# A pooled attention and gated convolution kernel: prologue reordered, groups of one at first, keys in 128-row chunks, and DMA transposes in place of TensorE's from sequence 2 on

## The chip, the cores and the metric

One core of a Trainium2 chip runs the whole program. The metric is device microseconds of one execution, the median of several. A profiled execution of the same kernel gives the trace from which all rows below are taken. PE is TensorE, PEld its weight loads, DVE VectorE, ACT ScalarE, POOL GpSimd, SP SyncE.

## The reference

There are 8 sequences of 576 positions, 8 heads of 64. Keys and values are averaged over blocks of 8 positions, so that each head has 72 pooled keys. The attention output of all heads (512 columns) goes through a gated feed-forward part with a convolution over three neighbouring positions.

```python
k_p = k.reshape(B, H, Sp, 8, D).mean(axis=3)        # Sp = 72
v_p = v.reshape(B, H, Sp, 8, D).mean(axis=3)
scores = q @ k_p^T / sqrt(D);  attn = softmax(scores);  x = attn @ v_p   # heads side by side: 576 x 512
h = relu(x @ w_in)                                   # 576 x 1024
conv[s] = sum over k of conv_w[k] * h[s + k - 1]     # three taps, zero at both ends
out = (h * sigmoid(conv)) @ w_out                    # 576 x 512
```

## The kernel before

All products are in bf16 with float32 sums in PSUM. Sequences are handled in `groups`, `[[0], [1, 2], [3, 4], [5, 6], [7]]`. A load brings a sequence's q or k to 64 partitions (row p holds the nine positions 9p to 9p+8), so a pair fills 128 partitions. A group has 5 tiles of query rows if it is one sequence (four of 128 rows and one of 64) and 9 if it is a pair (the middle one has 64 rows of each).

Preparation of a group: `prep_k` (L153) multiplies the key rows by a 0/1 pooling matrix `pm` that GpSimd builds, 72 matmuls in two halves, and DVE casts the sums to `kT` (L163). `prep_q` (L196) turns the queries on TensorE in five pieces, copied by DVE to `qT` (L202, L206, L211). `prep_v` adds the eight rows of each value block in three DVE steps (L172, L176, L179) into `va`, with 72 pooled positions on partitions and a ninth-of-65 column that holds 8, which yields the row sums.

Attention of a tile is five steps, `STEPS`:

1. `att_scores`: four matmuls of two heads each into the PSUM tile `s_ps` (L234; the pool `s_psum` has one buffer), and the negated row maxima `negm` on DVE (L243).
2. `att_exp`: two matmuls of an identity add `negm` to the scores (L257), then ACT takes the exponential into `e_t` (L266).
3. `att_transpose`: TensorE turns `e_t` head by head, eight transposes into `e_ps` (L277), and DVE copies them to `eT_t` (L283).
4. `att_values`: eight matmuls, one for each head, into `o_ps` (L293), then DVE's reciprocal (L302) and product `x_t` (L304).
5. `att_out`: TensorE turns `x_t` in four blocks (`x_ps`, L319), ACT copies them into `xT_t` (L324), the layout that the feed-forward part reads.

Feed-forward of a sequence: for each of eight blocks `fb`, `ffn_in` (8 matmuls, `h_ps` L338, relu on ACT L345), `ffn_conv` (8 or 10 matmuls by diagonal weights `dw`, `c_ps` L392, tanh on ACT L401) and `ffn_gate` (DVE, L410 and L411). `ffn_out` takes a tile through eight matmuls of 512 columns (`o_out` L419), an ACT copy (L427) and two DMAs to `out` from the SP queue (L435).

The order on every engine is written out by hand. The prologue loads on the POOL queue (k and q of 0, v of 0, `w_in`, k and q and v of 1, k and q of 2, `w_out`, v of 2, then the next pair), prepares group 0, runs the five steps over its five tiles, prepares group 1 and both its values. After that a plan of `SLOTS = 24` slots for each sequence b mixes the feed-forward part of b with the attention of b + 1, the preparation of the group that begins at b + 2, and the `ffn_out` tiles of b - 1. `at(slot, order, f)` puts a step in a slot; each engine runs its instructions in that order. A tile's five steps stand two slots apart. The pools `big_psum` and `sm_psum` (two buffers each) hold `h_ps`, `c_ps`, `o_ps` and all the small ones.

Of the kernel before, what the change touches and what calls it, by code (L numbers as in the profile page):

```python
# [16 lines left out]
def kernel(  # L17
# [21 lines left out]
    P = 128  # L39
# [7 lines left out]
    SLOTS = 24  # L47

    groups = [[0], [1, 2], [3, 4], [5, 6], [7]]
# [5 lines left out]
    v_pool = ctx.enter_context(tc.tile_pool(name="vp", bufs=2))  # L55
    vt_pool = ctx.enter_context(tc.tile_pool(name="vt", bufs=1))
    qT_pool = ctx.enter_context(tc.tile_pool(name="qT", bufs=2))
    att_pool = ctx.enter_context(tc.tile_pool(name="att", bufs=3))
    xT_pool = ctx.enter_context(tc.tile_pool(name="xT", bufs=2))
# [10 lines left out]
    ident_f = const.tile([P, P], FP32, name="ident_f")  # L70
    pm = const.tile([P, C, 2, Sp], BF16, name="pm")
    w_in_sb = [const.tile([P, d_ff], BF16, name=f"w_in_sb{c}") for c in range(n_dmc)]
# [4 lines left out]
    va_ring = [const.tile([Sp, H, D + 1], BF16, name=f"va{i}") for i in range(4)]  # L77
    kT_ring = [const.tile([P, n_pairs, KW], BF16, name=f"kT{i}") for i in range(4)]

    q_t, k_t, v_t, va_t, qT_t, xT_t, gT_t, hT_t = {}, {}, {}, {}, {}, {}, {}, {}  # L80
# [20 lines left out]
    def load_v(b):  # L101
        v_t[b] = v_pool.tile([Sp, H, POOL * D], BF16, name="v_t")
        nc.gpsimd.dma_start(
            out=v_t[b], in_=v[b].rearrange("h (sp r) d -> sp h (r d)", r=POOL)
        )

    def load_group(g):
        for i in range(len(groups[g])):
            load_k(g, i)
            load_q(g, i)  # L110
            load_v(groups[g][i])


    def build_pool_matrix():
        nc.gpsimd.memset(pm, 1.0)
        for base, sign in ((0, 1), (POOL - 1, -1)):
            nc.gpsimd.affine_select(
                out=pm,
                in_=pm,
# [3 lines left out]
                pattern=[[sign, C], [-sign * C * TB, 2], [-sign * POOL, Sp]],  # L123
                channel_multiplier=sign * C,
            )

    def build_conv_weights():
        cps = sm_psum.tile([P, 3 * n_fb], FP32, name="cw_ps", tag="sm")
# [16 lines left out]
    def prep_k(g, half):  # L145
# [3 lines left out]
        for j in range(2):  # L149
            pr = 2 * half + j  # L150
            for c in range(C):
                for hh in range(2):
                    nc.tensor.matmul(  # L153
                        out=ps[hh * D:(hh + 1) * D, j, 0:n, :],
                        lhsT=k_t[g][0:rows, 2 * pr + hh, c * D:(c + 1) * D],
                        rhs=pm[0:rows, c, 0:n, :],
# [11 lines left out]
    def prep_v(b):  # L168
        vt = v_t[b]
        va = va_ring[b % 4]  # L170
        t1 = vt_pool.tile([Sp, H, 4 * D], BF16, name="vt1")
# [3 lines left out]
        t2 = vt_pool.tile([Sp, H, 2 * D], BF16, name="vt2")  # L175
        nc.vector.tensor_tensor(  # L176
            out=t2, in0=t1[:, :, 0:2 * D], in1=t1[:, :, 2 * D:4 * D], op=OP.add
        )
        nc.vector.tensor_tensor(  # L179
            out=va[:, :, 0:D], in0=t2[:, :, 0:D], in1=t2[:, :, D:2 * D], op=OP.add  # L180
        )
        va_t[b] = va

    def prep_q(g, pr):

# [297 lines left out]
    with tc.manual_schedule():  # L483
# [20 lines left out]
        for kT in kT_ring:  # L504
            nc.vector.memset(kT, 0.0)
# [55 lines left out]
```

## Time and profile before

| | |
|---|---|
| median of three runs | 321.84 us (321.68 to 322.76) |
| profiled execution | 324.01 us, span 322.2 us |
| PE busy | 276.5 us, 86% of the span, 3087 matmuls |
| PEld / DVE / ACT / POOL busy | 201.5 / 177.6 / 145.0 / 27.0 us |
| granted TensorE clock | 0.989 of full speed |
| moved by DMA | 26.17 MB, HBM read 32.52 MB |

Times are counted from the first instruction of the span. A busy time of PE counts each matmul with its pipeline, so what a group of matmuls really takes from PE is read from the start of one group to the start of the next. The idle time of an engine is put down to whatever ended it.

### The profile page before, as it was taken

The page shows a single profiled execution, that of the slowest core. Times are in us where ns is not written, and L with a number is a line of the kernel's source. Part 1 is how long each engine was busy: PE and PEld are TensorE (multiplying, and loading weights), DVE is VectorE, ACT ScalarE, POOL GpSimd, SP SyncE. Part 2 cuts the span into 40 slices and gives each one's busy share as a digit, 9 for nine tenths or more (in the row PEclk, how much of TensorE's full clock was granted, in tenths as well). Part 3 has the DMA queues.
Part 4 walks back from the last instruction along what each step waited for, and adds up shares of the span by engine and source line. Part 5 has one row for each costly group of instructions (what it writes and reads, how often), then busy time and mean ns, then how long its engine had stood idle before and what let it go on. Part 6 is the DMA issues. An engine that isn't in the chain of part 4 may idle for free.

```text
span 322.2 us, 7171 instructions
## 1 busy us (share of the span) xinstructions
PE 276.5 (86%) x3087; PEld 201.5 (63%) x3087; DVE 177.6 (55%) x402; ACT 145.0 (45%) x240; POOL 27.0 (8%) x42
## 2 busy tenths in 40 slices
PE   0528782998999999998999999999999999989994
PEld 0526572786667666776676666766676677656651
DVE  3846558486387745655687636643864466432210
ACT  0022300465644455655544365556454556546442
POOL 8732004100020100000000000000000000000000
PEclk9999998799999999999999999999999999999999
DMA  7899999993139693111161121111102111302335
GB/s 108 110 198 181 170 191 144 175 177 64 35 41 185 106 194 68 35 33 35 35 108 33 37 56 30 43 40 33 34 16 54 33 35 35 67 2 65 67 67 112
DMA packets 22195, 26.17 MB, mean 81 GB/s; under 512 B 3196, under 2 KB 17044, under 8 KB 22164
## 3 DMA queue, kind: packets, MB, share of 16 engines
q0 software_dynamic: 16368, 16.26, 37.1%
q1 hardware_dynamic: 5796, 9.45, 12.9%
q8 instruction: 24, 0.39, 0.5%
q14 instruction: 7, 0.06, 0.1%
HBM read 32.52 MB, written 9.44 MB: 130 GB/s over the span
## 4 chain that ended last, share of the span: by engine, by line
PE 67%; DMA 13%; ACT 9%; DVE 5%; POOL 3%; issue 2%; ACTq 0%; POOLq 0%
PE h_ps L338 18%; PE o_out L419 17%; PE c_ps L392 16%; DMA v_t<-in_v_dram 9%; PE e_ps L277 5%; ACT tg_t L401 4%; DMA w_in_sb<-in_moe_w_in_dram 4%; ACT hT_t L345 3%; PE s_ps L234 3%; PE q_ps L196 2%; PE s_ps L257 2%; PE k_ps L153 2%; DVE gT_t L411 2%; PE x_ps L319 2%; DVE tg_t L410 1%
## 5 line engine op out<-in xcount | busy, mean ns | idle before, releaser
L338 PE MATMUL h_ps<-xT_t,w_in_sb 128*128 128x288 bf16 x512 | 75.4, 288 | 4.8 <-ACT xT_t L324 3.6
L419 PE MATMUL o_out<-w_out_sb,gT_t 128*128 128x512 bf16 (+1 forms) x296 | 70.9, 380 | 0.6
L345 ACT ACTIVATE hT_t<-h_ps 128x576 bf16<-128x576 f32 x64 | 41.6, 650 | 55.2 <-PE h_ps L338 54.1
L392 PE MATMUL c_ps<-hT_t,dw 128*128 128x288 bf16 (+4 forms) x560 | 58.3, 249 | 6.8 <-ACT hT_t L345 4.3
L338 PEld LDWEIGHTS <-w_in_sb 128*128 128x128 bf16 x512 | 48.3, 98 | 20.3 <-issue 5.8
L392 PEld LDWEIGHTS <-dw 128*128 128x128 bf16 x560 | 44.7, 98 | 17.6 <-issue 6.6
L401 ACT ACTIVATE tg_t<-c_ps 128x576 bf16<-128x576 f32 x64 | 41.7, 651 | 28.2 <-PE c_ps L392 27.4
L419 PEld LDWEIGHTS <-gT_t 128*128 128x128 bf16 (+1 forms) x296 | 26.9, 98 | 31.3 <-DVE gT_t L411 4.5
L427 ACT COPY osb_t<-o_out 128x512 f32<-128x512 f32 (+1 forms) x37 | 21.6, 585 | 46.2 <-PE o_out L419 46.2
L243 DVE TENSOR_REDUCE negm<-s_ps 128x8 bf16<-128x576 f32 (+1 forms) x37 | 27.8, 752 | 24.7 <-PE s_ps L234 24.5
L410 DVE TENSOR_SCALAR tg_t<-tg_t 128x576 bf16<-128x576 bf16 x64 | 19.5, 304 | 39.5 <-ACT tg_t L401 39.3
L283 DVE COPY eT_t<-e_ps 72x1024 bf16<-72x1024 bf16 (+1 forms) x37 | 24.8, 671 | 29.5 <-PE e_ps L277 29.4
L266 ACT ACTIVATE e_t<-s_ps 128x576 bf16<-128x576 f32 (+1 forms) x37 | 24.0, 650 | 16.5 <-PE s_ps L257 16.4
L411 DVE TENSOR_TENSOR gT_t<-tg_t,hT_t 128x576 bf16<-128x576 bf16 x64 | 29.3, 458 | 2.2
L304 DVE TENSOR_TENSOR x_t<-o_ps,r_t 128x512 bf16<-128x512 f32 (+1 forms) x37 | 25.6, 691 | 1.3
L277 PE MATMUL e_ps<-ident,e_t 128*72 128x128 bf16 (+1 forms) x296 | 24.4, 230 | 1.4 <-ACT osb_t L427 1.3
L257 PE MATMUL s_ps<-negm,ident 128*128 128x288 bf16 (+1 forms) x74 | 16.7, 311 | 10.2 <-DVE negm L243 10.2
L324 ACT COPY xT_t<-x_ps 128x512 bf16<-128x512 bf16 (+1 forms) x37 | 21.2, 572 | 5.5 <-PE x_ps L319 5.5
L277 PEld LDWEIGHTS <-e_t 128*72 128x72 bf16 (+1 forms) x296 | 20.3, 122 | 2.8 <-issue 1.7
L234 PE MATMUL s_ps<-kT,qT_t 128*128 128x144 bf16 (+1 forms) x160 | 16.9, 241 | 3.6 <-ACT e_t L266 3.6
L302 DVE RECIPROCAL r_t<-o_ps 128x8 f32<-128x8 f32 (+1 forms) x37 | 7.6, 206 | 18.4 <-PE o_ps L293 17.9
L293 PE MATMUL o_ps<-va,eT_t 72*128 72x65 bf16 (+1 forms) x320 | 17.4, 201 | 0.1
(38 smaller groups left out, 189.7 us busy)
## 6 DMA issues: line engine op xcount, KB each, us to landing
out_dram<-osb_t SPq DMA_DIRECT2D x72, 128.0 KB, 2.4
v_t<-in_v_dram POOLq DMA_DIRECT2D x8, 576.0 KB, 9.8
k_t<-in_k_dram POOLq DMA_DIRECT2D x7, 576.0 KB, 15.7
q_t<-in_q_dram POOLq DMA_DIRECT2D x7, 576.0 KB, 18.5
w_in_sb<-in_moe_w_in_dram POOLq DMA_DIRECT2D x4, 256.0 KB, 11.5
w_out_sb<-in_moe_w_out_dram POOLq DMA_DIRECT2D x1, 1024.0 KB, 26.3
k_t<-in_k_dram POOLq DMA_DIRECT2D x2, 288.0 KB, 4.5
q_t<-in_q_dram POOLq DMA_DIRECT2D x2, 288.0 KB, 5.2
```

The lines of the kernel that those rows point to most:

```text
L234: nc.tensor.matmul(out=sp[lo:hi, pr // 2, (pr % 2) * KW:(pr % 2 + 1) * KW], lhsT=qT_t[g][:, pr, t * P + lo:t * P + hi], rhs=kT_ring[b % 4] ...
L243: nc.vector.tensor_reduce(out=negm[0:rows], in_=sp[0:rows, :, 0:2 * KW].rearrange("p a (h s) -> p a h s", s=Sp), axis=AX.X, op=OP.max, neg ...
L266: nc.scalar.activation(out=e[0:rows], in_=sp[0:rows, :, 0:2 * KW], func=ACT.Exp, scale=1.0 / (POOL * 8.0))
L277: nc.tensor.transpose(out=ps[:, h, 0:rows], in_=e[0:rows, h // 4, (h % 4) * Sp:(h % 4 + 1) * Sp], identity=ident[0:rows, 0:rows],)
L283: nc.vector.tensor_copy(out=eT[:, :, 0:rows], in_=ps[:, :, 0:rows])
L304: nc.vector.tensor_tensor(out=x[0:rows].rearrange("p (a h d) -> p a h d", a=2, d=D), in0=ov[:, :, :, 0:D], in1=r[0:rows].unsqueeze(3).to_b ...
L338: nc.tensor.matmul(out=hps[:, j, 0:SC], lhsT=w_in_sb[dc][:, fb * P:(fb + 1) * P], rhs=xT_t[g][:, dc, i * S + j * SC:i * S + (j + 1) * SC], ...
L345: nc.scalar.activation(out=hT_t[b][:, fb, :].rearrange("p (a s) -> p a s", a=2), in_=hps[:, :, 0:SC], func=ACT.Relu, scale=0.5,)
L392: nc.tensor.matmul(out=cps[:, j, lo - j * SC:hi - j * SC], lhsT=dw[:, kk, fb, :], rhs=hT[:, fb, src:src + hi - lo], start=(kk == 1), stop= ...
L401: nc.scalar.activation(out=tg.rearrange("p (a s) -> p a s", a=2), in_=cps[:, :, 0:SC], func=ACT.Tanh, scale=0.5)
L411: nc.vector.tensor_tensor(out=gT_t[g][:, fb, i * S:(i + 1) * S], in0=tg1, in1=hT_t[b][:, fb, :], op=OP.mult)
L419: nc.tensor.matmul(out=ops_[0:rows, :], lhsT=gT_t[g][:, fb, t * P:t * P + rows], rhs=w_out_sb[:, fb, :], start=(fb == 0), stop=(fb == n_fb ...
```

## The change

Groups are `[[0], [1], [2], [3], [4, 5], [6, 7]]`. The loads stand in another order on the POOL queue and are spread over the plan. The exponentials of a tile lie in one 640-column row (eight heads of 72 and 64 zero columns) and are turned in five chunks of 128 pooled keys; values lie likewise in five chunks of 128 rows, with three masked copies, so that a chunk's matmul writes all heads that it meets. From sequence 2 on (`E_DMA`, `X_DMA`) both turns are `dma_start_transpose` on the SP queue. The first sequence's scores use two PSUM tiles in turn. The matmuls of sequence 0's `ffn_in` go by halves of the sequence. The plan's slots are other ones.

```diff
+    NJ = 5
+    KP = NJ * P
+    E_DMA = 2
+    X_DMA = 2
-    groups = [[0], [1, 2], [3, 4], [5, 6], [7]]
+    groups = [[0], [1], [2], [3], [4, 5], [6, 7]]
...
-    va_ring = [const.tile([Sp, H, D + 1], BF16, name=f"va{i}") for i in range(4)]
+    v_ring = [const.tile([P, NJ, POOL * D], BF16, name=f"v{i}") for i in range(2)]
+    vm_ring = [const.tile([P, NJ, 3, D + 1], BF16, name=f"vm{i}") for i in range(4)]
+    e_ring = [const.tile([P, KP], BF16, name=f"e{i}") for i in range(4)]
     kT_ring = [const.tile([P, n_pairs, KW], BF16, name=f"kT{i}") for i in range(4)]
...
     def load_v(b):
-        v_t[b] = v_pool.tile([Sp, H, POOL * D], BF16, name="v_t")
+        rows = v[b].rearrange("h (sp r) d -> (h sp) (r d)", r=POOL)
+        vt = v_ring[b % 2]
         nc.gpsimd.dma_start(
-            out=v_t[b], in_=v[b].rearrange("h (sp r) d -> sp h (r d)", r=POOL)
-        )
-    def load_group(g):
-        for i in range(len(groups[g])):
-            load_k(g, i)
-            load_q(g, i)
-            load_v(groups[g][i])
-    def build_pool_matrix():
-        nc.gpsimd.memset(pm, 1.0)
+            out=vt[:, 0:4, :], in_=rows[0:4 * P].rearrange("(j p) x -> p j x", p=P)
+        )
+        nc.gpsimd.dma_start(out=vt[0:TB, 4, :], in_=rows[4 * P:])
...
+    def build_head_mask():
+        nc.gpsimd.memset(mask, 1.0)
+        for base, sign in ((Sp, 1), (-1, -1)):
+            nc.gpsimd.affine_select(
+                out=mask,
+                in_=mask,
+                compare_op=OP.is_ge,
+                fill=0.0,
+                base=base,
+                pattern=[[sign * (P - 2 * Sp), NJ], [-sign * Sp, 3]],
+                channel_multiplier=sign,
+            )
+        for vm in vm_ring:
+            nc.vector.tensor_scalar(
+                out=vm[:, :, :, D], in0=mask, scalar1=float(POOL), scalar2=None, op0=OP.mult
...
-        vt = v_t[b]
-        va = va_ring[b % 4]
-        t1 = vt_pool.tile([Sp, H, 4 * D], BF16, name="vt1")
+        vt = v_ring[b % 2]
...
+        t3 = vt_pool.tile([P, NJ, D], BF16, name="vt3")
         nc.vector.tensor_tensor(
-            out=va[:, :, 0:D], in0=t2[:, :, 0:D], in1=t2[:, :, D:2 * D], op=OP.add
-        )
-        va_t[b] = va
+            out=t3, in0=t2[:, :, 0:D], in1=t2[:, :, D:2 * D], op=OP.add
+        )
+        nc.vector.tensor_tensor(
+            out=vm_ring[b % 4][:, :, :, 0:D],
+            in0=t3.unsqueeze(2).to_broadcast([P, NJ, 3, D]),
+            in1=mask.unsqueeze(3).to_broadcast([P, NJ, 3, D]),
+            op=OP.mult,
...
+            copy = nc.scalar.copy if g == 0 and pr % 2 else nc.vector.tensor_copy
+            copy(out=qT[:, pr, 0:8 * TB].rearrange("p (c t) -> p c t", t=TB), in_=ps[:, :, 0:TB])
...
-        sp = s_psum.tile([P, 2, 512], FP32, name="s_ps")
+        if g == 0 and t % 2:
+            sp = big_psum.tile([P, 2, 512], FP32, name="s_ps", tag="big")
+        else:
+            sp = s_psum.tile([P, 2, 512], FP32, name="s_ps")
...
-        e = att_pool.tile([P, 2, 2 * KW], BF16, name="e_t")
+        e = e_ring[tile_no[g, t] % 4]
         nc.scalar.activation(
-            out=e[0:rows], in_=sp[0:rows, :, 0:2 * KW], func=ACT.Exp, scale=1.0 / (POOL * 8.0)
+            out=e[0:rows, 0:4 * KW].rearrange("p (a x) -> p a x", a=2),
+            in_=sp[0:rows, :, 0:2 * KW],
+            func=ACT.Exp,
+            scale=1.0 / (POOL * 8.0),
...
-        ps = sm_psum.tile([Sp, H, P], BF16, name="e_ps", tag="sm")
-        for h in range(H):
+        eT = eT_pool.tile([P, NJ, P], BF16, name="eT_t")
+        a["eT"] = eT
+        if groups[g][0] >= E_DMA:
+            nc.sync.dma_start_transpose(out=eT[:, :, 0:rows], in_=e[0:rows, :])
+            return
+        ps = sm_psum.tile([P, NJ, P], BF16, name="e_ps", tag="sm")
+        for j in range(NJ):
             nc.tensor.transpose(
-                out=ps[:, h, 0:rows],
-                in_=e[0:rows, h // 4, (h % 4) * Sp:(h % 4 + 1) * Sp],
+                out=ps[:, j, 0:rows],
+                in_=e[0:rows, j * P:(j + 1) * P],
                 identity=ident[0:rows, 0:rows],
             )
-        eT = att_pool.tile([Sp, H, P], BF16, name="eT_t")
-        nc.vector.tensor_copy(out=eT[:, :, 0:rows], in_=ps[:, :, 0:rows])
-        a["eT"] = eT
+        copy = nc.scalar.copy if g == 0 else nc.vector.tensor_copy
+        copy(out=eT[:, :, 0:rows], in_=ps[:, :, 0:rows])
...
-            for h in range(H):
+            for j, x0, x1, first in (
+                (0, 1, 3, True), (1, 0, 3, False), (2, 0, 1, False),
+                (2, 1, 3, True), (3, 0, 3, False), (4, 0, 1, False),
+            ):
+                h = 2 * j - 1 + x0
+                kk = P if j < 4 else TB
                 nc.tensor.matmul(
-                    out=o[lo:hi, h // 4, (h % 4) * (D + 1):(h % 4 + 1) * (D + 1)],
-                    lhsT=eT[:, h, lo:hi],
-                    rhs=va_t[b][:, h, :],
-                    start=True,
-                    stop=True,
+                    out=o[lo:hi, h // 4, (h % 4) * (D + 1):(h % 4 + x1 - x0) * (D + 1)],
+                    lhsT=eT[0:kk, j, lo:hi],
+                    rhs=vm_ring[b % 4][0:kk, j, x0:x1, :],
+                    start=first,
+                    stop=(j == 4 or (j == 2 and x0 == 0)),
+                    skip_group_check=True,
...
+        if groups[g][0] >= X_DMA:
+            nc.sync.dma_start_transpose(
+                out=xT_t[g][:, :, t * P:t * P + rows], in_=a["x"][0:rows, :]
+            )
+            return
...
+    def ffn_in_half(b, j, f2):
+        g, i = where[b]
+        if b not in hT_t:
+            hT_t[b] = hT_pool.tile([P, n_fb, S], BF16, name="hT_t")
+            gT_t[g] = gT_pool.tile([P, n_fb, 2 * S], BF16, name="gT_t")
+        hps = big_psum.tile([P, 2, 512], FP32, name="h_ps", tag="big")
+        for f in range(2):
+            fb = 2 * f2 + f
+            for dc in range(n_dmc):
+                nc.tensor.matmul(
+                    out=hps[:, f, 0:SC],
+                    lhsT=w_in_sb[dc][:, fb * P:(fb + 1) * P],
+                    rhs=xT_t[g][:, dc, j * SC:(j + 1) * SC],
+                    start=(dc == 0),
+                    stop=(dc == n_dmc - 1),
...
+        if b == 0:
+            for j in range(2):
+                for f2 in range(n_fb // 2):
+                    at(w + 4 * j + f2, 0, ffn_in_half, b, j, f2)
+            for r in range(n_fb):
+                at(w + 6 + 2 * r, 0, ffn_conv, b, r)
+                at(w + 7 + 2 * r, -1, ffn_gate, b, r)
...
+            e_dma, x_dma = groups[ng][0] >= E_DMA, groups[ng][0] >= X_DMA
+            first = 5 if b == 0 else 0
+            m4 = 6 if e_dma else 5
+            steps = (0, 2, 2 if e_dma else 3, m4, m4 if x_dma else m4 + 2)
+            gap = (22.9 - first - steps[4] - (3 if x_dma else 0)) / (len(ts) - 1)
             for n, t in enumerate(ts):
-                s = w + int(n * gap)
+                s = w + first + int(n * gap)
                 for m, f in enumerate(STEPS):
-                    at(s + 2 * m, 1 + (4 - m), f, ng, t)
-        lead = [g2 for g2 in range(1, len(groups)) if groups[g2][0] == b + 2]
-        for g2 in lead:
-            for half in range(2):
-                at(w + 8 + 2 * half, 7, prep_k, g2, half)
-            for n2 in range(n_pairs + 1):
-                at(w + 12 + 2 * n2, 7, prep_q, g2, n2)
-            for n2, b2 in enumerate(groups[g2]):
-                at(w + 7 + 8 * n2, 8, prep_v, b2)
-            if g2 + 1 < len(groups):
-                at(w + 23, 9, load_group, g2 + 1)
+                    at(s + steps[m], 1 + (4 - m) if not (m == 2 and e_dma or m == 4 and x_dma) else 6,
+                       f, ng, t)
+            if ni == 0:
+                for n2, b3 in enumerate(groups[ng]):
+                    at(w + (7 if b == 0 else 1 + 2 * n2), 8, prep_v, b3)
+        for g2 in range(1, len(groups)):
+            b2 = groups[g2][0]
+            if b2 == b + 2:
+                for half in range(2):
+                    at(w + 11 + 2 * half, 7, prep_k, g2, half)
+                for n2 in range(n_pairs + 1):
+                    at(w + 14 + 2 * n2, 7, prep_q, g2, n2)
+            if b2 == b + 3 and g2 > 2:
+                for n2, b3 in enumerate(groups[g2]):
+                    at(w + 6 + 8 * n2, 9, load_k, g2, n2)
+                    at(w + 9 + 8 * n2, 9, load_q, g2, n2)
+        if b >= 3 and i == 0:
+            for n2, b3 in enumerate(groups[g]):
+                at(w - 2 * SLOTS + 2 + 6 * n2, 9, load_v, b3)
...
     with tc.manual_schedule():
         load_k(0, 0, slice(0, 4))
         load_k(0, 0, slice(4, 8))
         load_q(0, 0, slice(0, 4))
         nc.sync.dma_start(out=cw_raw, in_=moe_conv_w.rearrange("k (fb p) -> (k fb) p", p=P))
+        load_q(0, 0, slice(4, 8))
         make_identity(nc, ident)
-        build_pool_matrix()
-        make_identity(nc, ident_f)
-        load_q(0, 0, slice(4, 8))
+        nc.vector.memset(warm, 0.0)
+        nc.scalar.activation(out=warm, in_=warm, func=ACT.Exp)
+        for v0 in v_ring:
+            nc.vector.memset(v0[TB:P, 4, :], 0.0)
+        build_pool_matrix(True)
         load_v(0)
         for c in range(n_dmc):
             nc.gpsimd.dma_start(out=w_in_sb[c], in_=moe_w_in[c * P:(c + 1) * P, :])
+        for kT in kT_ring:
+            nc.vector.memset(kT, 0.0)
+        build_conv_weights()
+        build_head_mask()
+        for e in e_ring:
+            nc.vector.memset(e[:, 4 * KW:], 0.0)
         load_k(1, 0)
         load_q(1, 0)
         load_v(1)
-        load_k(1, 1)
-        load_q(1, 1)
+        build_pool_matrix(False)
+        for half in range(2):
+            prep_k(0, half)
+        for pr in range(n_pairs + 1):
+            prep_q(0, pr)
+        load_k(2, 0)
+        load_q(2, 0)
         nc.gpsimd.dma_start(
             out=w_out_sb, in_=moe_w_out.rearrange("(fb p) d -> p fb d", p=P)
         )
-        for kT in kT_ring:
-            nc.vector.memset(kT, 0.0)
-        for va in va_ring:
-            nc.vector.memset(va, float(POOL))
-        build_conv_weights()
-        prep_k(0, 0)
-        prep_k(0, 1)
-        for pr in range(n_pairs + 1):
-            prep_q(0, pr)
-        prep_v(0)
         ts = tiles_of[0]
-        for s in range(len(ts) + 4 + len(ts)):
+        for s in range(len(ts) + 4):
             for m in reversed(range(5)):
-                n, odd = divmod(s - m, 1)
-                if 0 <= n < len(ts):
-                    STEPS[m](0, ts[n])
-        for half in range(2):
-            prep_k(1, half)
-        for pr in range(n_pairs + 1):
-            prep_q(1, pr)
-        prep_v(1)
+                if 0 <= s - m < len(ts):
+                    STEPS[m](0, ts[s - m])
+            if s == 1:
+                prep_v(0)
+            if s == 4:
+                for half in range(2):
+                    prep_k(1, half)
+            if s > 4:
+                prep_q(1, s - 5)
+        prep_q(1, n_pairs)
         load_v(2)
-        prep_v(2)
-        load_group(2)
         for key in sorted(plan):
```

## The prediction

> **What bounds the kernel now.** I read four views in this order: the span in forty slices, the chain that ended last, PE's order of time in a steady stretch, and PE's waits. The slices say that there are two stages.
>
> ```profile
> PE   0528782998999999998999999999999999989994
> PEclk9999998799999999999999999999999999999999
> ```
>
> One digit is 8.1 us. PE is full from slice 8 (about 57 us) to the last slice but one, and half idle before. The chain of the first 60 us says why the full stretch starts there:
>
> ```profile
> 23.70 29.82 DMA v_t<-in_v_dram
> ...
> 53.55 1.23 DVE vt L172
> ...
> 55.95 0.68 DVE negm L243
> ...
> 56.66 0.64 PE s_ps L257 x2
> 57.30 1.92 PE h_ps L338 x8
> ```
>
> The load of sequence 2's values lands at 53.5 us; `prep_v(2)` waits for it on DVE, and behind it in DVE's order stands the `negm` that the first interleaved tile needs. PE reached its feed-forward part at 49.43 us, did 1.3 us of it and stood. It resumes at 56.66, so the stage counts from 55.4. The eight matmuls of 57.30 take 1.92 us; the same group takes 0.99 later, since the granted clock is 0.50 from 54 to 60 us.
>
> In the steady stretch what a group takes from PE is the distance to the next start (start, duration, engine, line):
>
> ```profile
> 96.14 0.90 PE L392 MATMUL c_ps<-hT_t,dw 128*128 128x288 bf16 x8
> 96.88 0.42 PE L293 MATMUL o_ps<-va,eT_t 72*128 72x65 bf16 x8
> 97.23 1.32 PE L153 MATMUL k_ps<-pm,k_t 128*64 128x144 bf16 x36
> 98.48 0.42 PE L257 MATMUL s_ps<-negm,ident 128*128 128x288 bf16 x2
> 98.74 1.14 PE L338 MATMUL h_ps<-xT_t,w_in_sb 128*128 128x288 bf16 x8
> 99.72 0.39 PE L319 MATMUL x_ps<-ident,x_t 128*128 128x128 bf16 x4
> ...
> 101.36 0.62 PE L277 MATMUL e_ps<-ident,e_t 128*72 128x128 bf16 x8
> 101.81 1.89 PE L419 MATMUL o_out<-w_out_sb,gT_t 128*128 128x512 bf16 x8
> 103.53 0.41 PE L234 MATMUL s_ps<-kT,qT_t 128*128 128x144 bf16 x4
> ```
>
> So c 0.74, values 0.35, half a pair's keys 1.25, negm 0.26, h 0.98, x turn 0.23 to 0.31, e turn 0.45 to 0.53 (other places), out 1.73, scores 0.25 to 0.35. Groups follow each other without gaps: PE is the bound. What it waits for after the resumption is little, 12.6 us in all (waiter, releaser, us, times, longest):
>
> ```profile
> PE c_ps L392 <- ACT hT_t L345: 4.3, 11, 0.5
> PE h_ps L338 <- ACT xT_t L324: 3.6, 7, 0.6
> PE c_ps L392 <- DVE x_t L304: 2.2, 4, 0.5
> PE e_ps L277 <- ACT osb_t L427: 1.3, 3, 0.4
> ```
>
> **Prologue: 55.4 becomes 37.** The first scores come at 16.64 us. They follow the kT casts, which DVE does after 24 `dw` products. After the change DVE has some 2.7 us more of small fills ahead of the casts, but starts the products 3.5 us earlier, since the identity that they wait for no longer follows GpSimd's pooling matrix: I leave 16.64. Before, the first `negm` waits for `prep_v(0)` (and that for the values, landed 18.5) and ends at 21.57; now it precedes it and ends at 17.75. From 21.57 to the last xT copy's end, 41.40, five tiles take 19.8 us. In this stretch 3.6 us of PE waits for ACT's exponential to free the one score buffer go, as the tiles alternate between two; the table load of 1.3 us is done in advance; `prep_v(0)` now keeps back the first values (+1.8 of its 2.3 us). Sequence 1's keys and queries now stand between the tiles: 5.1 us of PE by the rows of sequence 0 (2.37 and 2.73), half of it in PE's idle time (PE is busy 13.9 of the 20 us from 20 to 40): +2.6. Sum 17.75 + 19.8 - 3.6 - 1.3 + 1.8 + 2.6 = 37.05. Below: rounds paced by ACT alone (0.65 + 0.65 + 0.58 a tile), nine of them from 16.64, 33.6. Above: no step shortened and all of the preparation exposed, 21.57 + 19.8 + 5.1 = 46.5. The pair's separate preparation, both `prep_v` and the wait for `v_t` leave the path. The transfers cover this: sequence 1's queries are the seventh of 590 KB-sized pieces in a queue that brought 4.0 MB by 28 us, before they are used. GpSimd's second pooling matrix (two of 1.41 us) now stands ahead of the loads of sequence 2; megabytes queued before it hide it, and without that cover it would cost 2.8 us of a landing that is not wanted until slot 11. Gain 18.4, and the stretch at half clock (0.38 + 0.93 + about 0.3 in its groups): 1.6.
>
> **PE work.** The turns of 28 tiles leave PE: 28 x (0.48 + 0.26) = 20.7 us (19.0 by the shortest distances, 28.6 by the full durations 0.62 and 0.40). Sequence 1's five tiles turn five chunks instead of eight: 5 x 3 x 0.057 = 0.9. Values: six matmuls of 780 columns for eight of 520; at 288 columns in 0.122 us that is 0.33 for 0.35, nothing. Against it: sequences 2 and 3 are prepared singly (3.1 each by sequence 7's: two halves of 0.7, four pieces of 0.37, one of 0.24), so preparations after the prologue are 2 x 3.1 + 2 x 5.0 for 5.0 + 5.0 + 3.1: +3.1. One tile more (38 for 37): 0.86 and an `ffn_out` of 1.73: +2.6. Net -15.9. DVE's 28 copies of 0.685 and ACT's 28 of 0.584 go too, at no gain of their own: neither is the bound (55% and 45%). `ffn_in` of sequence 0 by halves is the same 64 matmuls.
>
> **Waits.** Of the 12.6 us those tied to the removed turns go (3.6 + 2.2 + 1.3): -7.1. In their place comes the landing of a DMA transpose, which no row shows. Nearest is the same queue's `out` transfer, 128 KB against 164 KB (e) and 131 KB (x):
>
> ```profile
> DMA to landing us min/median/max: 2.2/2.4/9.6
> ```
>
> (us from issue to landing of the 72 `out` transfers.) I take 3.0, near the median, with one neighbour's issue (0.51) ahead of it; ends 2.2 and 9.6. On SP, queued behind each transpose's wait for ACT or DVE, are the `out` pairs and the next tile's transposes, 56 more issues beside 72. From the changed program's order, priced by the distances above, I sum the PE work between a tile's negm matmuls and its value matmuls: eight of the 28 tiles have 2.9 to 3.3 us, the others 4.0 to 7.7, mean 4.6. The chain there is exponential 0.65, ACT's queue and signals 0.35, landing 3.0: 4.0. It is short in the eight, by 6.7 us together. The turned x must be there for the next sequence's `ffn_in`: six such joints have 2.5 to 4.8 us of cover against 0.21 + 0.69 + 0.1 + 3.0 = 4.0; short by about 2.0. New waits 8.7.
>
> [...]
>
> Sum against the profiled execution: 322.2 - 18.4 - 1.6 - 15.9 - 7.1 + 8.7 = 287.9 us of span, 289.7 with the 1.8 around it. The profiled execution lies 2.2 above the median of the runs, so 287.5, say 288.
>
> **Rivals.** (1) The prologue is bound by arrival and chain, not by what I took off: PE's stage starts at 46.5, time 298. For it: the DMA engines are busy without a break from 8 to 72 us in the slices. Against: what is needed first is loaded first. (2) The transposes land in 4 us, as SP's queue holds them up: chain 5.0, shortfall 19.5 at the values and 5 at the joints for 8.7: 304. (3) Slower: the transposes are the bound. One mechanism: each landing beyond PE's cover stops PE in its order, tile by tile. At a landing of 4.6 us (chain 5.6) the shortfalls are 32 and 9 us, the gain of 34 is used up and the time is as before; at 6 us they are 69 and 17, and the time is 365. For it: the transposes share the queue with 72 transfers, one of which took 9.6. Against: the median of 2.4. That the turns do not leave PE is ruled out: of 37 groups of e turns the changed program has 10.
>
> **Chances.** Forecast as it stands (277 to 296) 0.62; rival 1 0.13; rival 2 0.13; slower 0.11; no change 0.01. Faster by over 0.3%, which is about what a measurement can tell here: 0.88. The range's low end takes a prologue of 34, the turns at their full durations and no e shortfall: 288 - 3 - 4 - 4 = 277. Its high end takes in rival 1 with some late transposes and half of rival 2: 306. Left out are slower and half of rival 2.
>
> **What would show it.** Right: PE full from slice 5; `v_t` gone from the chain; no L277 or L319 group after about 90 us; transposes landing in 2.4 to 3.5 us; PE's waits on them under 10 us. Wrong: value matmuls waiting for `eT_t` a microsecond or more in most tiles; SP's transposes taking over 2 us each to issue; a first `ffn_in` after 45 us.

## The result and the profile after

The changed kernel takes 332.89 us (median of 331.33 to 337.43), the kernel before 322.30 beside it: a ratio of 1.031, 95% interval 1.024 to 1.037. It is slower; 288 was predicted. The profiled execution took 331.33 us, span 329.5, granted clock 0.963 (0.989 before). An execution more than 1.5% above the fastest of its kernel counts as slow and is left out of the ratios, not of the medians.

The span in forty slices, 8.2 us each:

```profile
PE   1569968880999752999797998999788889999994
PEclk9999999996799995899979999999999999999999
```

PE is busy from slice 4 on, as predicted, but has holes in slices 10, 15 to 16 and 22, and a smaller one in 20. The clock is 0.50 from 76.4 to 86.6 us and from 124.2 to 134.4, in and behind the first two holes, and from 165.1 to 168.5, behind the one in slice 20. The chain that ended last (start, us, what) names the three large holes:

```profile
34.93 5.99 PE h_ps L414 x48
...
72.18 9.92 DMA eT_t<-e
...
117.81 11.56 DMA eT_t<-e
...
170.13 6.54 DMA eT_t<-e
```

The feed-forward part starts at 34.93 us, and `v_t` is gone from the chain. In its place stand e turns of 6.5 to 11.6 us where 3.0 was counted. PE's waits (waiter, releaser, us, times, longest) agree:

```profile
PE o_ps L339 <- DMA eT_t<-e: 24.9, 9, 9.6
PE o_out L495 <- DVE gT_t L487: 6.5, 3, 2.3
...
PE o_ps L339 <- DVE eT_t L325: 2.1, 1, 2.1
```

Before, all of PE's waits after the resumption were 12.6 us; here they are 40.0 from 35.5 us on. The landings of the e turns (26 of the 28 have one in the trace), min, median and max:

```profile
DMA to landing us min/median/max: 2.3/2.6/14.4
```

The median is what was predicted. The long ones stand together, and POOL's timeline shows beside what (the e turns on SP are issued at 72.18 and 74.0, and land after 9.9 and 10.8 us):

```profile
67.53 0.68 POOL L96 DMA_DIRECT2D q_t<-in_q_dram  x1 [10.70 <-PE q_ps L228]
68.19 0.68 POOL L105 DMA_DIRECT2D k_t<-in_k_dram  x1
...
70.38 0.77 POOL L113 DMA_DIRECT2D v<-in_v_dram  x1 [0.83 <-DVE vt L198]
```

The plan's slots don't spread the loads: POOL has nothing else to do and issues each as soon as its buffer is free, which is when the preparation of the group before ends. That is also when the next sequence's first tile is turned. Set beside the loads in flight, the 26 e turns fall into two kinds: 19 with no load in flight have a median of 2.6 us (one is over 4), and seven beside loads have 2.9 to 14.4, median 9.9.

The windows of 74, 76 and 84 us (stretch, length, busy us of PE, PEld, DVE, ACT, POOL, granted clock, DMA share, GB/s) show what follows:

```profile
74.00:76.00 2.00, 0.28 (x3) 0.00 (x0) 0.25 (x1) 0.65 (x1) 0.00 (x0) 1.00 1.15 223
76.00:78.00 2.00, 0.00 (x0) 0.00 (x0) 0.00 (x0) 0.00 (x0) 0.00 (x0) 0.60 1.18 225
...
84.00:86.00 2.00, 2.00 (x10) 1.14 (x9) 0.82 (x3) 0.65 (x1) 0.00 (x0) 0.50 0.37 77
```

From 76 to 78 us all four engines stand while the DMA engines move 225 GB/s (DMA share 1.18), and when PE resumes at 82.15 us it runs four microseconds at half clock, to 86.6.

The second and third of the waits above come from VectorE's order. In the trace of after, around the end of sequence 1's stage:

```profile
113.44 1.16 DVE L209 TENSOR_TENSOR vm<-vt,mask 128x960 bf16<-128x960 bf16 x1
114.51 0.46 DVE L486 TENSOR_SCALAR tg_t<-tg_t 128x576 bf16<-128x576 bf16 x1
115.00 0.46 DVE L487 TENSOR_TENSOR gT_t<-tg_t,hT_t 128x576 bf16<-128x576 bf16 x1
```

`prep_v` (four instructions, 2.8 us) stands in slot 1 of the next stage, ahead of the last gate `gT_t` of this one, for which `ffn_out` waits; in sequence 0's stage it stands ahead of an `eT_t` copy.

### The profile page after: what moved, and what is told of

Read it like the earlier page. It is cut to its first block, busy times and chain, and to the rows that moved or that the text cites. A ratio compares the mean times of both kernels' runs of the same rounds, so it can differ in the third digit from the quotient of the medians.

```text
span 329.5 us, 6716 instructions
## 1 busy us (share of the span) xinstructions
PE 269.4 (82%) x2791; PEld 184.4 (56%) x2791; DVE 162.4 (49%) x390; ACT 138.2 (42%) x223; POOL 31.4 (10%) x52
## 4 chain that ended last, share of the span: by engine, by line
PE 64%; DMA 15%; DVE 11%; ACT 3%; issue 3%; POOL 3%; ACTq 0%; POOLq 0%
PE o_out L495 17%; DMA eT_t<-e 14%; PE h_ps L390 14%; PE c_ps L468 12%; PE o_ps L339 6%; PE s_ps L268 3%; PE q_ps L228 3%; PE s_ps L291 3%; PE h_ps L414 2%; PE k_ps L179 2%; DVE vm L209 2%; DVE gT_t L487 2%; DVE x_t L351 1%; DVE vt L198 1%; ACT tg_t L477 1%
## 5 line engine op out<-in xcount | busy, mean ns | idle before, releaser
L495 PE MATMUL o_out<-w_out_sb,gT_t 128*128 128x512 bf16 (+1 forms) x304 | 74.5, 388 | 6.8 <-DVE gT_t L487 6.5
L390 PE MATMUL h_ps<-xT_t,w_in_sb 128*128 128x288 bf16 x448 | 65.3, 289 | 1.0 <-DMA xT_t<-x_t 1.0
L477 ACT ACTIVATE tg_t<-c_ps 128x576 bf16<-128x576 f32 x64 | 41.6, 650 | 54.1 <-PE c_ps L468 51.9
L390 PEld LDWEIGHTS <-w_in_sb 128*128 128x128 bf16 x448 | 42.4, 98 | 16.5 <-DMA xT_t<-x_t 1.5
L339 PE MATMUL o_ps<-vm,eT_t 128*128 128x130 bf16 (+5 forms) x240 | 26.2, 231 | 29.5 <-DMA eT_t<-e 24.9
L495 PEld LDWEIGHTS <-gT_t 128*128 128x128 bf16 (+1 forms) x304 | 28.1, 101 | 39.3 <-DVE gT_t L487 10.2
L397 ACT ACTIVATE hT_t<-h_ps 128x576 bf16<-128x576 f32 x56 | 36.4, 650 | 31.6 <-PE h_ps L390 30.9
L339 PEld LDWEIGHTS <-eT_t 128*128 128x128 bf16 (+1 forms) x240 | 17.4, 103 | 40.1 <-DMA eT_t<-e 29.1
L300 ACT ACTIVATE e<-s_ps 128x576 bf16<-128x576 f32 (+1 forms) x38 | 24.7, 651 | 8.4 <-PE s_ps L291 8.4
L268 PE MATMUL s_ps<-kT,qT_t 128*128 128x144 bf16 (+1 forms) x160 | 17.9, 244 | 1.8 <-ACT e L300 1.8
L228 PE MATMUL q_ps<-ident,q_t 64*64 64x64 bf16 (+1 forms) x432 | 16.2, 211 | 3.8 <-DVE kT L190 3.5
L228 PEld LDWEIGHTS <-q_t 64*64 64x64 bf16 (+1 forms) x432 | 12.3, 115 | 8.0 <-issue 6.4
L113 POOL DMA_DIRECT2D v<-in_v_dram x8 | 6.1, 768 | 106.9 <-DVE vt L198 104.7
## 6 DMA issues: line engine op xcount, KB each, us to landing
w_in_sb<-in_moe_w_in_dram POOLq DMA_DIRECT2D x4, 256.0 KB, 10.8
w_out_sb<-in_moe_w_out_dram POOLq DMA_DIRECT2D x1, 1024.0 KB, 19.9
```

What stands on the lines that cost most here:

```text
L228: nc.tensor.transpose(out=ps[hh * D:(hh + 1) * D, j, 0:rows], in_=q_t[g][0:rows, 2 * x + hh, c * D:(c + 1) * D], identity=ident[0:rows, 0: ...
L268: nc.tensor.matmul(out=sp[lo:hi, pr // 2, (pr % 2) * KW:(pr % 2 + 1) * KW], lhsT=qT_t[g][:, pr, t * P + lo:t * P + hi], rhs=kT_ring[b % 4] ...
L339: nc.tensor.matmul(out=o[lo:hi, h // 4, (h % 4) * (D + 1):(h % 4 + x1 - x0) * (D + 1)], lhsT=eT[0:kk, j, lo:hi], rhs=vm_ring[b % 4][0:kk, ...
L390: nc.tensor.matmul(out=hps[:, j, 0:SC], lhsT=w_in_sb[dc][:, fb * P:(fb + 1) * P], rhs=xT_t[g][:, dc, i * S + j * SC:i * S + (j + 1) * SC], ...
L397: nc.scalar.activation(out=hT_t[b][:, fb, :].rearrange("p (a s) -> p a s", a=2), in_=hps[:, :, 0:SC], func=ACT.Relu, scale=0.5,)
L477: nc.scalar.activation(out=tg.rearrange("p (a s) -> p a s", a=2), in_=cps[:, :, 0:SC], func=ACT.Tanh, scale=0.5)
```

## The experiments

Times are medians beside runs of the kernel before on the same chip (322.9 to 323.4).

| kernel | us | ratio to before, 95% interval |
|---|---|---|
| light_loads | 326.7 | 1.007 (1.002 to 1.012) |
| x_only | 323.3 | none given (before 323.1) |
| e_only | 337.4 | 1.040 (1.032 to 1.049) |
| no_dma_turns | 332.8 | 1.021 (1.011 to 1.031) |
| x_vbank | 316.9 | 0.978 (0.972 to 0.984) |
| x_prepv | 305.2 | 0.943 (0.937 to 0.949) |
| paced | 339.9 | 1.041 (1.030 to 1.053) |
| all_paced | 328.9 | 1.014 (1.006 to 1.023) |
| x_k128 | 299.8 | 0.929 (0.924 to 0.934) |
| none_k128 | 319.1 | 0.988 (0.982 to 0.995) |
| all_k128 | 325.3 | 1.008 (1.004 to 1.012) |
| paced8_k128 | 328.7 | 1.019 (1.012 to 1.026) |
| all_noload | 303.2 | 0.941 (0.935 to 0.946) |
| x_noload | 305.4 | 0.946 (0.941 to 0.951) |
| e_late | 298.7 | 0.926 (0.922 to 0.931) |

### Fewer bytes, and one kind of turn at a time

light_loads, edits to the loads of sequences 3 to 7:

```diff
+            if groups[g][0] >= 3:
+                nc.gpsimd.memset(q_t[g], 0.01)
         b = groups[g][i]
+        if b >= 3:
+            heads = slice(0, 1)
...
+        if b < 3:
+            nc.gpsimd.dma_start(
```

(The first two edits stand in the loads of q and k alike; the last one is around the load of the first four chunks of v.)

> From sequence 3 on, seven of eight heads of q and k and the first four chunks of v are not loaded (zeros-like filler or older data stand there), so some 1.5 MB less is in flight per sequence; every other instruction stays. Theory A, loads in flight hold up the DMA transposes and through them PE: the e turns that took 9.9, 11.6 and 14.4 us land in 2.6, PE's waits for eT_t fall from 24.9 us to some 5, the half-clock stretches behind the long waits go too, and the time falls by 22 to 28 us to about 306. Theory B, the first transposes of a stretch are slow by themselves or by SP's order: the time stays within 3 us of the changed kernel's 332.9 and the long landings stay where they are.

Waits on `eT_t` fell from 24.9 to 13.0 us, the longest from 9.6 to 3.8, the longest landing from 14.4 to 5.9. Fewer bytes shorten the late turns; yet the time is still above the kernel before. The run also has some 4 us of waits on VectorE that the changed kernel hasn't (on `gT_t` 9.0 for 6.5 us, and 1.6 on an `eT_t` copy), beside GpSimd's filling of q and k, so the time understates what the bytes are worth. Even so, late turns are one part only.

x_only is `E_DMA = 8` (exponentials on TensorE), e_only is `X_DMA = 8` (attention output on TensorE), no_dma_turns has both.

> E_DMA = 8: exponentials are turned on TensorE in five chunks for all sequences, only the attention output is turned by DMA. Theory A (late e turns are what costs): no value matmul waits for a DMA, -25 us of waits and -6 us of half clock, +28 x 0.29 = 8 us of PE work: 308 to 312. Theory C (the groups of one, the new order and the values in 128-row chunks cost the time, not the turns): no gain against the changed kernel beyond 5 us, so 328 or more. x turns may land late beside loads, but only the last tile's is near its use.

> X_DMA = 8: the exponentials go by DMA as in the change, the attention output is turned on TensorE again. Theory A: the late e turns stay, and 28 x 0.24 = 7 us of PE work comes back, part of it inside the waits: 332 to 340. If instead the x turns held up the e turns on SP's queue, the time falls below 325.

> E_DMA = X_DMA = 8: no DMA transposes, all else of the change stays (prologue, groups, 128-row chunks, plan). Theory A: waits and half clock gone (-31), PE work of both turns back (+8 and +7): 312 to 318, still faster than before the change by the shorter prologue. Theory C: 328 or more.

e_only has 23.0 us of waits on `eT_t` from DMA, x_only and no_dma_turns none. The gain and the loss separate: x turns by DMA gain 9.5 us here (332.8 to 323.3; 7.5 in span, 327.3 to 319.8), e turns by DMA lose 9.6 (323.3 to 332.9; 9.7 in span, 319.8 to 329.5). e_only came as theory A had it, no_dma_turns as theory C, and x_only between the two. For without any DMA transpose the new form is still 2.1% slower than the kernel before, some 7 us, though its feed-forward part starts 14 us earlier (34.98 for 49.43). Something else costs some 21 us. Its 6.5 us of waits on `gT_t` were the first clue.

### VectorE's order, and the value matmuls

x_prepv is x_only with `prep_v` one slot later in its stage, and in the first stage six slots earlier:

```diff
-                    at(w + (7 if b == 0 else 1 + 2 * n2), 8, prep_v, b3)
+                    at(w + (1 if b == 0 else 2 + 2 * n2), 8, prep_v, b3)
```

> The kernel is x_only with one edit: the value preparations on VectorE stand one slot later in their stage (slot 2 instead of 1, and slot 1 instead of 7 in the first sequence), so that they no longer stand ahead of the last gate of the sequence before (or of the e copy). Theory D (VectorE's order makes the stops): the three waits of L495 on gT_t (6.5 us) and the wait of 2.1 us of the value matmuls at 50 us go, and with the stop at 50 us the stretch at half clock behind it (51 to 62 us, some 5 us lost): 323 falls to 311 to 316. Rival (the value preparation then stands ahead of another copy which PE needs as soon, and the half clock comes for another reason): waits of the same sum under another name, granted clock still 0.5 at 51 to 62 us, 322 to 324 us.

305.2 us, 18 less than x_only's median and 15.9 less in span (319.8 to 303.9), more than any theory gave. The waits on `gT_t` are gone, that on `eT_t` fell to 0.3 us, and the granted clock is 1.00 in every stage (0.964 over x_only's span). Of the 15.9 us, 8.8 are waits. The rest, 7.1, fits the half clock, which x_only has from the stop at 50 us to about 61, and again behind three others: PE works 19.7 us at it, which can cost up to 9.9, an estimate by half of that time: in x_only a group of `ffn_in` takes 1.87 us from start to start at 0.50 (112.34 us) and 0.99 at 1.00 (105.93 us).

x_vbank is x_only with the six value matmuls in another order:

```diff
-                (0, 1, 3, True), (1, 0, 3, False), (2, 0, 1, False),
-                (2, 1, 3, True), (3, 0, 3, False), (4, 0, 1, False),
+                (0, 1, 3, True), (2, 1, 3, True), (1, 0, 3, False),
+                (3, 0, 3, False), (2, 0, 1, False), (4, 0, 1, False),
```

> The kernel is x_only (exponentials turned on TensorE, attention output by DMA) with one edit: the six value matmuls of a tile alternate between the two PSUM banks of o_ps, so that no matmul adds into columns that the one just before it wrote, but for one pair. In x_only the six take about 0.55 us a tile from start to start, where before eight of 65 columns took 0.35; six of 195, 195, 130, 130, 65 and 65 columns at the 0.44 ns a column of o_out and the 42 ns least of the old value matmuls would take about 0.37. Theory V (adding into the columns just written stalls the next matmul): o_ps falls from about 92 to about 62 ns a matmul, 0.37 us a tile, 36 tiles by 0.18 = 6.5 us, 317 us for x_only's 323. Rival (the price goes with the weight loads and the columns streamed, whatever their order): o_ps stays at 92 ns, 323 us.

The time agrees with theory V, 316.9, but the profile doesn't: a value group still takes 0.54 us (0.55 before the edit), and the starts only move their surplus to another pair. What differs is the clock. Both kernels have the same three stops of 2.1 to 2.3 us for `gT_t`; behind each of them x_only's clock is 0.50 for 3.4 us, x_vbank's is 1.00. In all, PE works 19.7 us at half clock in x_only and 6.6 in x_vbank; half of the difference is 6.6 us, and the spans differ by 6.3 (319.8 to 313.5). So V falls.

The traces also show where the same stop tells and where it does not. The stretches between two changes of the granted clock are whole multiples of 3.41 us: 6.83 in the kernel before (53.2 to 60.0 us), 10.24, 37.55, 10.24, 30.72 and 3.41 in the changed kernel (76.4 to 168.5 us), and by the windows 10.2 in x_only (51.0 to 61.2 us) and 6.8 in x_vbank (50.2 to 57.0 us). That is an observation of these four; no run tests a grid by itself. Cut into pieces of 3.41 us from one of these changes on, each of x_only's three stops lies whole in one piece, in which PE is busy for 1.1 to 1.3 us; each of x_vbank's crosses an edge, and PE is busy for 1.4 to 1.5 us of the piece that holds most of it. The first of the three in x_only, its piece and the next (columns as above), then in x_vbank:

```profile
109.00:112.40 3.40, 1.12 (x7) 0.46 (x6) 2.70 (x5) 0.11 (x1) 3.24 (x5) 1.00 0.46 63
112.40:115.80 3.40, 3.40 (x22) 2.48 (x21) 0.82 (x2) 1.68 (x3) 0.82 (x2) 0.50 1.11 154
```

```profile
108.20:111.60 3.40, 1.42 (x11) 0.99 (x11) 1.89 (x3) 0.99 (x2) 3.34 (x6) 1.00 0.81 117
111.60:115.00 3.40, 3.40 (x35) 2.56 (x34) 2.06 (x6) 2.10 (x4) 0.00 (x0) 1.00 1.13 169
```

The starts inside a group told where the surplus sits: 57, 88, 33, 60, 181 and 130 ns. 98 ns too much stand ahead of the last matmul and 97 behind it, and this one alone contracts over 64 rows. x_k128 is x_prepv with

```diff
-                kk = P if j < 4 else TB
+                kk = P
```

> The kernel is x_prepv (305.2) with one edit: the last of the five value chunks is contracted over 128 rows like the other four (its upper 64 rows are zeros) instead of over 64. In x_prepv the starts of a tile's six value matmuls lie 57, 88, 33, 60, 181 and at least 130 ns apart: 98 ns above the 83 of 195 columns ahead of the 64-row matmul, and 97 above its 33 behind it; x_vbank moved the first surplus (83, 126 against 33) with the order, and took none away. Theory K (a change between 128 and 64 contracted rows costs about 97 ns each way): both surpluses go, 36 tiles by 0.19 = 7 us, o_ps from 96 to about 62 ns a matmul, 305 falls to 298 (297 to 300). Rival (the surplus belongs to the place in the accumulation, or to the end of the group): starts stay as they are, 304 to 306.

299.8 us, 5.4 less of the 7 expected. One value group and what follows it in x_prepv (start, us, line), then the same in x_k128:

```profile
112.21 0.62 PE L339 MATMUL o_ps<-vm,eT_t 128*128 128x130 bf16 x6
112.76 1.15 PE L390 MATMUL h_ps<-xT_t,w_in_sb 128*128 128x288 bf16 x8
```

```profile
109.65 0.52 PE L339 MATMUL o_ps<-vm,eT_t 128*128 128x130 bf16 x6
110.00 1.14 PE L390 MATMUL h_ps<-xT_t,w_in_sb 128*128 128x288 bf16 x8
```

From start to start 0.55 against 0.35. Both surpluses went (the starts are now 57, 88, 33, 60, 87 and 31 ns), so theory K holds. A change from 128 to 64 contracted rows, and the change back, cost about 97 ns each here; no run shows what the time goes into. The kernel before contracted over 72 rows in all of these matmuls, and its eight starts lie 33 ns apart.

x_k128 in slices:

```profile
PE   2369888899999999999899999999899899999993
PEclk9999999999999999999999999999999999999999
```

No hole, no half clock.

### Loads at other times

paced is the changed kernel with the loads of sequences 4 to 7 held back until a given part of `hT` is written:

```diff
+    def gated(b, r, f, *args):
+        nc.gpsimd.tensor_copy(out=gate_t, in_=hT_t[b][0:1, r, 0:2])
+        f(*args)
...
-                    at(w + 6 + 8 * n2, 9, load_k, g2, n2)
+                    at(w + 9, 9, gated, b, 3, load_k, g2, 0)
```

(and so on for the other q, k and v loads, to about one every 3 to 7 slots). all_paced adds the edits of x_prepv and x_vbank.

> The kernel is the changed kernel with the loads of q, k and v for groups from the fourth on each held back on GpSimd until a given row of hT is written (a copy of two elements ahead of the load), so that a burst of five loads is spread over the stage: same bytes, same transposes, other times. Theory A (DMA transposes that are issued while 4 to 6 loads are under way land after 6 to 14 us): waits of L339 on eT_t fall from 24.9 to under 8 us, longest landing from 14.4 to under 6, half clock at 78 to 86 us and 124 to 134 us gone; the time falls from 333 by 17 + 8 = about 25, to 305 to 312. light_loads, which took the bytes away, gave 326.7 with 13.0 us of these waits, so by the part of it that bytes alone give: 325. Rival (late turns come of the covers, of SP's issue or of ACT, not of the loads' times): waits of 20 us or more on eT_t, 330 to 335.

> The three edits of x_vbank, x_prepv and paced put together on the changed kernel (exponentials by DMA again). If theories A, V and D all hold and add up: 333 - 25 (late turns and their half clock) - 6.5 (value matmuls) - 8 (VectorE's order) = about 294, that is the predicted 288 less the terms that were missed. If V fails: 300. If A fails (turns late whatever the loads): 318 or more. Rival of all: the stops only change their names, and the time stays above 322, the kernel before.

Theory A's remedy fails, and its mechanism shows why. In paced (rows of its longest execution, 347.5 us) no e turn takes over 6.8 us, but 20 transposes now meet a load (9 in the changed kernel), of which 18 take over 4; with none in flight the medians are 2.6 and 2.4 as ever. The waits on `eT_t` are 24.5 us, as in the changed kernel, and those on `xT_t` are 5.7 (1.0 there). Spreading turned few long delays into many of a middle length, each just beyond the cover. all_paced, profiled at 330.4 us, has 21.6 and 6.3, and there too 20 transposes meet a load, of which 17 take over 4.

### The two turns priced without the other losses

none_k128 is x_k128 with `X_DMA = 8`, all_k128 with `E_DMA = 2`; paced8_k128 is all_k128 with the loads of paced and `m4 = 8` (values two slots later).

> The kernel is x_k128 with the attention output turned on TensorE again, so no DMA transposes at all, with the new prologue, groups of one and 128-row chunks. It prices the x turns by DMA alone, free of VectorE's order. no_dma_turns against x_only was 332.8 against 323.3, 9.5 us; the predicted price of the work moved was 28 tiles by 0.26 = 7.3. Theory (the x turns by DMA are a gain of their price on TensorE and cost no wait): x_k128 + 7 to 10, 305 to 308 if x_k128 comes to 298. Rival (part of the 9.5 came from ACT and VectorE stops that the place of prep_v made): x_k128 + 3 or less, 301.

> The changed kernel with the edits of x_prepv and x_k128: exponentials and attention output both by DMA, loads as the change has them. The changed kernel took 332.9. VectorE's order gave x_only 18 us, the 64-row chunk should give 7. If the e turns' waits are a separate sum: 333 - 18 - 7 = 308, some 10 above x_k128's 298, that is the late turns (25 us of stops, and their half clock) less 13 of TensorE work taken off. If the stops share their half clock with VectorE's, less is gained: 315. Rival (with the other stops gone the e turns by DMA pay as predicted): 298 - 28 * 0.48 + 8 of waits = 292 or less.

> all_k128 with the spread loads of paced, and with the value matmuls of a tile two slots later (step 8 instead of 6), so that an e turn has about 2 slots, 2.6 us, more cover. In paced no transpose took over 8.1 us (6 to 7 beside a load in flight, 2.6 with none), but about 20 of 56 met a load instead of 9, and the longest waits on eT_t were 3 to 4.3 us. Theory A' (a transpose beside a load takes 6 to 7 us, one beside none 2.6; what counts is the cover against that): waits on eT_t fall from 21.7 (all_paced) to under 6, the waits of h_ps on xT_t stay at about 6, no half clock but near those: 302 to 308, against all_k128's 308 or more. Rival (the later values only move the stop to the x turns and the first ffn_in): eT_t and xT_t waits together above 18, 315 or more.

The x turns by DMA are worth 19.3 us (319.1 to 299.8), twice the theory: 8.5 of TensorE time, and 7.2 more of waits in none_k128 than in x_k128, about half behind ACT (which makes 28 copies of 0.58 us less in x_k128) and half behind VectorE. The other 3.6 are not split. The prediction had called ACT's copies no gain of their own.

The e turns by DMA cost 25.5 us (299.8 to 325.3), more than any theory gave. all_k128's wait:

```profile
PE o_ps L339 <- DMA eT_t<-e: 30.3, 12, 8.3
```

TensorE gets 9.4 us back (e_ps 10.9 to 1.5) and stands 30 for it, and it works 17.9 us at half clock, where x_k128 has none. A likely reason for the 5 us more than in the changed kernel, not tested by itself, is that with the other stops gone PE arrives earlier at the same transfers.

More cover (paced8_k128) does what A' says to `eT_t`, 1.4 us of wait, and loses it elsewhere, the rival's way:

```profile
PE h_ps L390 <- DMA xT_t<-x_t: 17.7, 5, 6.7
PE s_ps L268 <- ACT e L300: 13.0, 14, 1.1
```

### Are the loads the whole of it?

all_noload and x_noload are all_k128 and x_k128 without the loads of sequences 3 to 7:

```diff
+        if b >= 3:
+            return
```

> all_k128 without the q, k and v loads of sequences 3 to 7 (q and k are filled with a constant by GpSimd, v keeps the values of an earlier sequence), so that the e turns meet stores only. Theory L (loads in flight are the whole reason for the late e turns): no landing over 4.5 us, waits on eT_t of 8 us or less (those of 1.3 to 1.8 that all_k128 has after 190 us), granted clock 1.0 throughout, and a time within 4 us of x_noload's. Rival (covers, SP's issue or ACT's queue make them late as well): waits above 15 us, half clock somewhere, more than 8 us above x_noload.

> x_k128 without the same loads: the measure for all_noload. Its TensorE hardly waits for loads (0.8 us for xT_t), so it should stay at x_k128's time, 296 to 300; if it falls below 294, the loads cost x_k128 something that its waits don't name.

For the long waits, yes. In all_noload no landing is over 4.4 us and the wait is

```profile
PE o_ps L349 <- DMA eT_t<-e: 8.3, 9, 1.9
```

(the edit shifts the lines by ten), 8.3 for the 30.3 of all_k128, and the time is 2.2 us below x_noload's: theory L, though the waits are a little over its 8 us and the clock is 0.983 and not the 1.0 that it expected. The expectation for x_noload missed: it is 5.5 us slower than x_k128. A stop of 1.45 us on a VectorE copy at 60 us, 2.4 us of waits on `gT_t` and half clock from 34.3 to 37.7 us are new in it. GpSimd's filling of q and k is the one thing added, but no run tells which way it acts. The pair is therefore compared with each other and not with x_k128.

e_late keeps all the loads and turns only the last group's exponentials by DMA (`E_DMA = 6`), when no load is left.

> x_k128 with one edit: the exponentials of the last group (9 tiles, sequences 6 and 7) are turned by DMA, where no q, k or v load is under way any more. TensorE loses 9 turns of 0.34 us (x_k128's 10.9 us of e_ps against all_k128's 1.5, over 28 tiles) = 3.1 us. Theory (a turn that lands in 2.6 us still arrives 1.3 to 1.8 us after TensorE is ready for it in the first tile or two of a stage, as all_k128 shows at 268 and 286 us): 3.1 of work against 3 of waits, 298 to 301, no difference from x_k128. Rival (with no load in flight the turn pays its whole price): 297 or less. If the waits bring the half clock: 302 or more.

298.7 against 299.8, intervals of the ratios overlapping: no difference, as the theory had it, 2.2 us of waits against some 3 of work. e_late and x_k128 beat both kernels, by 7% the one before.

## Why the prediction was wrong

The sum said 287.9 us of span; 329.5 came. Step by step:

- **Prologue, 55.4 to 37.** Right, and 2.1 better: 34.93. Rival 1 (46.5) fell.
- **Turns off TensorE, -20.7 and -0.9.** Right: e turns went from 15.2 to 1.5 us of PE and x turns from 7.8 to 1.6, together -19.9. But x_k128's e turns take 10.9 us on TensorE: 4.3 of the 13.7 come from five chunks in place of eight, whoever turns them. The DMA's own part is 9.4.
- **"Values: nothing" (0.33 for 0.35).** Mis-sized: it counted columns and not the change from 128 to 64 contracted rows and back, about 97 ns each. A group took 0.55; the value matmuls went from 11.8 to 20.4 us, +8.6. x_k128 shows 5.0 of it (20.2 in x_prepv, 15.2 in x_k128); the rest no run splits.
- **Preparations, +3.1.** Keys and queries went from 13.6 to 18.0 us: +4.4.
- **VectorE.** "Neither is the bound" was true and not enough: the order had to be read. `prep_v` was taken off the prologue's path, and not followed to where it went, ahead of a gate: 8.6 us of waits, and with their half clock the 15.9 of span that x_prepv got back from x_only.
- **New waits, 8.7, with a landing of 3.0.** This is the step that failed most: 25.9 us on `eT_t` and `xT_t`. The shortfall of 6.7 from a chain of 4.0 was sound: all_noload has 8.3. What failed was the single landing taken from the median of a row with two kinds in it. The row already showed 2.2/2.4/9.6. Split by time, the trace of before gives for the two `out` transfers at 93 us, beside three loads, and then for those between 232 and 300 us, beside none:

```profile
DMA to landing us min/median/max: 7.2/8.4/9.6
```

```profile
DMA to landing us min/median/max: 2.2/2.3/2.5
```

  In all, eight `out` transfers of before met a load and took 2.7 to 9.6 us, median 6.4; 55 met none, median 2.4. The change puts the first turns of a stage where the loads start.
- **Clock.** The sum let the half clock in the prologue go and brought in none. The stops brought it back: 0.963 for 0.989.

Of the 41.6 us that the sum is short of, late transposes are 17.2 (25.9 less 8.7), VectorE's order 8.6, values 8.6, less 2.1 of the prologue. The 9.3 left are preparations (1.3), the turns (1.7 less gained than the 21.6 summed), matmuls at half clock and small waits; they are not split further. PE works 12.9 us at half clock in the changed kernel, which can cost up to 6.4 by the same estimate of one half. What half clock can cost is shown by x_prepv against x_only: 7.1 us of span beyond the waits that went (15.9 less 8.8), at a clock of 1.0 for 0.964.

Rival 3, the slower one, had the mechanism and the sign, and "one of which took 9.6" was its evidence. It had the wrong shape: not every landing somewhat longer, but two stops of 7.9 and 9.6 us beside bursts of loads, which make 17.5 of the 24.9, and seven short ones. Rival 2's "SP's queue holds them up" fell: an issue takes 1.2 us in the median, and with no load beside them the medians of the landings stay at 2.4 to 2.6.

Where no load is in flight, a turn of five 128x128 blocks lands in 2.6 us (median), beside the 2.4 of `out`. That did not settle which of the two turns gains by DMA: the exponentials lost 25.5 us by it, the attention output gained 19.3.

## What to carry to other kernels

Before a step is given to a DMA queue, split the landing times of its neighbours by what else is in flight: price the step by the row that it will stand beside, not by the median (here 6.4 us beside a load and 2.4 beside none, in a row with a median of 2.4). An engine that isn't the bound can still stop the one that is (here VectorE, busy for 49% of the span, stopped TensorE for 8.6 us), so follow each moved step to the instruction that it now stands ahead of. A short stop can cost more than its length where the clock falls behind it, as it did for 3.4 us behind x_only's stops of 2.1 to 2.3 us, and not behind x_vbank's of the same length at other times, so several small stops are to be removed together.

## What the runs showed of the hardware

- In the changed kernel a DMA transpose of 164 KB landed in 2.6 us (median) with no load in flight, in 2.9 to 6.5 beside one to three loads of 64 or 512 KB, and in 9.9 to 14.4 beside four to six loads of up to 576 KB issued together. No run shows what in the queues makes it late.
- A change of contraction from 128 to 64 rows between the value matmuls cost about 97 ns, and as much back (x_prepv against x_k128).
- The granted clock changed after whole multiples of 3.41 us (the kernel before, the changed kernel, x_only and x_vbank). Behind the same three stops of 2.1 to 2.3 us it fell to 0.50 where one such piece held the whole stop, with PE busy for 1.1 to 1.3 us of it (x_only), and stayed at 1.00 where the stop crossed an edge, with PE busy for 1.4 to 1.5 us (x_vbank).
